# One tiling fewer on TensorE: full-array matmuls issued as two halves of 64 columns

## The chip, the core and the metric

The kernel runs on one core of one Trainium2 chip. The core has a matmul engine (TensorE, called PE in the profile; its weight loads are listed apart as PEld), a vector engine (DVE), a scalar engine (ACT), a general engine (POOL) and a queue engine (SP) that here only issues DMA transfers. Matmuls write to PSUM, which has eight banks of 512 fp32 columns on 128 partitions; DVE and ACT copy ("evict") results from there to the on-chip memory. The metric is the device time of one execution in microseconds (us), a median of three runs for the kernel before. A profiled execution is a run of its own with its own time.

## What is computed

`x` is 8 x 4224 x 192 in fp32. The first part is a causal convolution along the sequence with 7 taps; the 192 channels form 8 groups of 24, and each group has its own softmax-normalised taps. The second part mixes tokens. Cut to what matters:

```python
x = conv(x, softmax(weight))                 # 7 taps, one set for each group of 24 channels
wq, wk = x @ w_q, x @ w_k                    # 192 -> 64 each
W_tok = (1 / sqrt(64)) * einsum('bsd,btd->bst', wq, wk)
mixed = einsum('bst,btd->bsd', W_tok, x)     # no softmax between
out = maximum(mixed, 0) @ w_out              # 192 -> 192
```

As nothing nonlinear stands between the two einsums, `mixed` equals `wq @ (w_k.T @ (x.T @ x))` up to the scale. The kernel uses this: it forms the 192 x 192 Gram matrix `x.T @ x` of each batch and never the 4224 x 4224 token matrix.

## The kernel before, in words

All matmuls are in bf16. Work goes batch by batch through these steps, each an operation on PE with an eviction behind it on ACT or DVE:

- `conv` (`gen_conv`, L559): the sequence is cut into 35 chunks of 122 outputs. For each of 8 channel groups a banded 128 x 128 matrix (`band`) multiplies the loaded chunks (`xw`), 9, 8, 18 or 17 chunks at once. Result: `y`, tokens on partitions.
- `tr_lo` and `tr_hi` (L598, L633): transposes of `y` through PE; the lower 128 channels take the full array, the upper 64 go to one half of the PE columns each for two parts of the sequence. Results: `ytl`, `yth`.
- `wq` (L658, L662): the queries, two blocks of 512 tokens side by side on the two column halves. Result: `wqt`.
- `gram` (L694): three matmuls per chunk on column halves, accumulated in an eighth PSUM bank over the whole batch. Then `turn` (L720) and `m` (L737), the small products with `w_k` that make the mixing matrices `msb` and `mbd`.
- `mix_lo` (L784), on the two row halves of the array, and `mix_hi` (L795), full array; their evictions apply the maximum with zero and write `rt`.
- `fin_hi` (L835, row halves) and `fin_lo` (L853, full array): the product with `w_out`, 128 tokens at a time. The stationary operand is `rt`, of which each matmul takes every fourth column, so that one partition of the output holds four rows that follow each other. `out_sb` is evicted (L869) and stored by SP (L877).

So PE is used in three tilings: 128x128 (full), 128x64 (`COL2`, two column halves that hold their own weights and take their own streams) and 64x128 (`ROW2`, two row halves). A short last block of 128 tokens uses 64x64 once per batch.

The order on each engine is not written by hand. Each operation is added with a planned length, what it needs, how many PSUM banks it takes (of seven) and a turn `vt`. `Planner.plan` places operations one after the other: on each engine, of those that are ready, the one with the smallest `vt`. `vt` comes from a formula of batch and position and an offset per kind from the table `TURN`. For PE, an operation in another tiling than the last one is ranked `STAY` = 0.8 later, waits of up to `HOLD` = 1 ns are accepted for one in the same tiling, and a change costs `SWITCH` = 95 ns of planned time. `Program.place` then writes each engine's stream with semaphore waits for what is not known to be done.

At the start, POOL issues the loads of `x`, which convert to bf16 on the way: batch 0 in four groups, each other batch in two, with a semaphore per group. SP issues nine transfers for the three weight matrices (`emit_weights`, L503) once the third load of batch 0 is in. They share one semaphore. Ten ACT copies (`cast`, L508) convert them to bf16; each of `wq`, `m`, `fin_hi` and `fin_lo` needs all ten (`*casts`). DVE makes the taps, and PE sums the bands with an identity as weights (`collect`, L423).

Of the kernel before, what the change touches and what calls it, by code (L numbers as in the profile page):

```python
# [8 lines left out]
BF16 = mybir.dt.bfloat16  # L9
F32 = mybir.dt.float32  # L10

FULL, COL2, ROW2 = "128x128", "128x64", "64x128"


class Op:


    n = 0

    def __init__(self, engines, emit, ns, needs=(), after=(), banks=0, drains=None, vt=0.0, mode=FULL, tail=0.0):  # L20
        self.engines = (engines,) if isinstance(engines, str) else tuple(engines)
        self.emit = emit

        self.ns = ns

        self.needs = [x for x in needs if x is not None]

        self.after = [x for x in after if x is not None]
        self.banks = banks

        self.drains = drains
        self.vt = vt
        self.mode = mode
        self.tail = tail
        self.users = 0
        self.bank = None
        self.engine = None
        self.end = None

        self.lands = 0.0  # L40

        self.size = 0
        Op.n += 1
        self.id = Op.n


class Planner:
# [1 line left out]


    LAT = {"PE": 240.0, "ACT": 145.0, "DVE": 140.0, "POOL": 150.0, "SP": 0.0}
    SWITCH = 95.0

    STAY = 0.8

    HOLD = 1

    def __init__(self, nbank, first_bank):
        self.ops = []
# [163 lines left out]
def bass_lightweight_conv__then__hypermixer_token_mlp_kernel(  # L223
# [87 lines left out]
    def bank(i, n=1):  # L311
        return PS[:, i * 512 : (i + n) * 512]


    TURN = {
        None: -0.36, "conv": -0.39, "fin_hi": 0.2, "fin_lo": -0.13, "g": -0.29, "gram": 0.01, "gt": 0.37,
        "m": -0.33, "mix_hi": 0.08, "mix_lo": -0.01, "ms": 0.64, "out": -0.7, "rh": -0.7, "rt": 0.7,
        "tr_hi": -0.04, "tr_lo": 0.25, "turn": 0.08, "wq": 0.02, "wqt": 0.3, "y": 0.08, "yth": 0.19,
        "ytl": 0.7,
    }  # L320

    def add(*a, dma=None, kind=None, **k):
        op = Op(*a, **k)
        op.dma = dma
        op.kind = kind
        op.vt += TURN.get(kind, 0.0)
        return planner.add(op)

    def evac_ns(cols, fast=1):
        return {"ACT": 56 + cols / 1.2, "DVE": 62 + cols / (0.96 * fast)}  # L330

    both = ("ACT", "DVE")


    S_W = semaphore("s_w")
# [7 lines left out]
    )  # L343

    one = add("DVE", lambda e, op: e.memset(IDENT[:, :], 1.0), 100, vt=-9.5)
    zero_yt = add("DVE", lambda e, op: e.memset(YTH[64:128, wq_cols[-2] :], 0.0), 100, vt=-8.52)
    zero_b = add("DVE", lambda e, op: e.memset(BAND[:, :, CW:128], 0.0), 80, vt=-8.9)
    zero_x0 = add("DVE", lambda e, op: e.memset(XW[0 : KC - 1, :, 0, :], 0.0), 800, vt=-8.8)
# [56 lines left out]
    for h0, nh in ((0, HB), (HB, HB)):  # L405
        fill, acc = None, None
        for k in range(KC):
            part = PARTS[:, at_part : at_part + CW * nh]
            at_part += CW * nh
            made = add(  # L410
                "DVE",
                lambda e, op, part=part, k=k, h0=h0, nh=nh: e.tensor_tensor(
                    part.rearrange("p (j h) -> p j h", h=nh),
                    IDENTW[:, k : k + CW, :],
                    WSB[:, k, h0 : h0 + nh].unsqueeze(1).to_broadcast([128, CW, nh]),
                    ALU.mult,
                ),
                360, needs=[wn, identw], vt=-7 + 0.1 * k + 0.2 * h0,
            )

            def collect(e, op, part=part, k=k, fill=fill):
                to = op if fill is None else fill
                return e.matmul(  # L423
                    bank(to.bank)[:, 0 : part.shape[1]], IDENT[:, :], part, start=k == 0, stop=k == KC - 1, skip_group_check=True
                )

            acc = add(
                "PE", collect, CW * nh / 2.4, needs=[made, ident], after=[acc], banks=1 if k == 0 else 0, vt=made.vt
            )
            fill = fill or acc  # L430
        done = add(
            "ACT",
            lambda e, op, h0=h0, nh=nh, fill=fill: e.copy(  # L433
                BAND[:, h0 : h0 + nh, 0:CW], bank(fill.bank)[:, 0 : CW * nh].rearrange("p (j h) -> p h j", h=nh)
            ),
            56 + CW * nh / 1.2,
            needs=[acc],
            drains=fill,
            vt=made.vt,
        )  # L440
        out_first.append(acc)
        for h in range(h0, h0 + nh):
            band_done[h] = done
# [47 lines left out]
        gen_load(0, gi)  # L491


    S_C = semaphore("s_c")
    QS, KS, OS = slice(0, DH), slice(DH, 2 * DH), slice(2 * DH, 2 * DH + D)

    def emit_weights(e, op):
        pairs = []
        for t, n, cols in ((wq_t, DH, QS), (wk_t, DH, KS), (wo_t, D, OS)):
            pairs.append((WLO[:, cols], bass.AP(t, 0, [[n, LO], [1, n]])))  # L500
            for p in (0, HI):
                pairs.append((WHI[p : p + HI, cols], bass.AP(t, LO * n, [[n, HI], [1, n]])))
        return [(e.dma_start(d, s), 16) for d, s in pairs]  # L503

    load_c = add("SP", emit_weights, 5000, needs=load[0, 2], dma=("c", S_C, 16 * 9), tail=2500, vt=-3)

    def cast(dst, src, more=()):
        return add("ACT", lambda e, op: e.copy(dst, src), 250, needs=[load_c, *more], vt=-4)  # L508

    def twice(ap):  # L510
        return ap.unsqueeze(1).to_broadcast([ap.shape[0], 2, DH])

    casts = [
        cast(WQL[:, :], WLO[:, QS]),
        cast(WQH[0:HI, 0, :], WHI[0:HI, QS], [zero_q]),
        cast(WQH[HI:128, 1, :], WHI[HI:128, QS], [zero_q]),
        cast(WKL[:, :, :], twice(WLO[:, KS])),
        cast(WKT[0:64, :, :], twice(WLO[0:64, KS]), zero_k),
        cast(WKM[0:64, :, :], twice(WLO[64:128, KS])),
        cast(WKM[64:128, :, :], twice(WHI[64:128, KS])),  # L520
        cast(WKB[64:128, :, :], twice(WHI[64:128, KS]), zero_k),
        cast(WOL[:, :], WLO[:, OS]),
        cast(WOH[:, :], WHI[:, OS]),
    ]

    for b in range(1, B):
# [17 lines left out]
    def gen_conv(b, gi):  # L544
# [6 lines left out]
        for hp in range(H // 2):  # L551
            vt = b + c0 / NCC - 0.15 + 0.02 * hp

            def conv(e, op, hp=hp):
                last = None
                for i in range(2):
                    h = 2 * hp + i
                    o = op.bank * 512 + i * gap
                    last = e.matmul(  # L559
                        PS[:, o : o + n * GRP],  # L560
                        BAND[:, h, :],
                        XW[:, b, c0 : c0 + n, GRP * h : GRP * h + GRP],
# [21 lines left out]
    def gen_transpose(b, cs):  # L584
# [8 lines left out]
        def tr_lo(e, op):  # L593
            ps = bank(op.bank).bitcast(BF16)
            last = None
            for c in cs:
                w, o = width[c], c * CW - t0
                last = e.transpose(ps[:, o : o + w], Y[0:w, yb, c, 0:LO], IDENT[0:w, 0:w])  # L598
            return last

        mm_l = add("PE", tr_lo, 57 * n, needs=needs, after=free, banks=1, vt=vt, kind="tr_lo")
# [10 lines left out]
    def gen_transpose_hi(b, j):  # L612
# [20 lines left out]
                    last = e.transpose(ps[64 * i : 64 * i + HI, o : o + w], Y[0:w, yb, c, LO:D], IDENT[0:w, 0:w])  # L633
            return last

        mm = add("PE", tr_hi, 55 * max(len(p) for p in parts), needs=needs, after=free, banks=1, vt=vt, mode=COL2, kind="tr_hi")
        y_read.setdefault((b, "all"), []).append(mm)
        return add(
            "DVE",
# [5 lines left out]
    def gen_wq(b, j):  # L645
# [8 lines left out]
        def wq(e, op):  # L654
# [9 lines left out]
                )  # L664
            return last

        mq = add("PE", wq, mm_ns(n, 2), needs=[*{id(r): r for c in cs for r in yt_done[b, c]}.values(), turned, *casts],
            after=wfree, banks=1, vt=vt, mode=COL2, kind="wq")
        yth_read[b, j] = [mq]
        for c in cs:  # L670
            for g in range(0, NCC, 8):
# [10 lines left out]
    def gen_gram(b, cs, first, last, before, begun):  # L682
# [18 lines left out]
                    )  # L701
            return mm

        a = add("PE", gram, 84 * len(cs), needs=[*needs, *before], after=begun, vt=vt, mode=COL2, kind="gram")
        y_read.setdefault((b, "all"), []).append(a)
        return [a]

    def gen_mix_weights(b, grams):
# [3 lines left out]
        def copy(dst, src):  # L712
# [4 lines left out]

        turn = add(
            "PE",
            lambda e, op: e.transpose(bank(op.bank).bitcast(BF16)[:, 0:LO], GSB[:, 64:D], IDENT[:, :]),  # L720
            60, needs=[g_read, ident], banks=1, vt=vt, kind="turn")
        turned = add(
            both,
# [3 lines left out]
        def m(e, op):  # L727
# [6 lines left out]
                (WKB, GSB[:, 0:64], LO),  # L734
            )
            for k, (wk, rhs, o) in enumerate(steps):
                last = e.matmul(  # L737
                    bank(op.bank)[:, o : o + rhs.shape[1]],
                    wk[:, :, :].rearrange("p t e -> p (t e)"),
                    rhs,  # L740
# [4 lines left out]
            return last  # L745

        gsb_read = mm = add(
            "PE", m, 290, needs=[g_read, turned, *casts], after=m_read.get(b - 2, []), banks=1, vt=vt, kind="m")
        mb = b % 2
        old = m_read.get(b - 2, [])  # L750

# [17 lines left out]
    def gen_mix(b, j, evm, evq):  # L769
# [5 lines left out]
        n_out += 1  # L775
        free = rt_read.get(n_rt - 1 - NRT, [])
        ofree = store_of[n_out - 1 - NOUT] if n_out > NOUT else out_first
        vt = b + 1.2 + t0 / S * 0.95 + (TURN.get(None, 0.0) if b == B - 2 else 0.0)
        nt = n // 128

        def mix_lo(e, op):
# [9 lines left out]
            return last  # L791

        def mix_hi(e, op):
            p = 64 * nh
            return e.matmul(  # L795
                bank(op.bank)[0:p, 0:n], MBD[0:p, mb, 0:p], WQT[0:p, wqb, q0 : q0 + n], start=True, stop=True
            )

        ml = add("PE", mix_lo, mm_ns(n), needs=[*evm, evq], after=free, banks=nh, vt=vt, mode=ROW2, kind="mix_lo")
        mh = add("PE", mix_hi, mm_ns(n), needs=[*evm, evq], after=free, banks=1, vt=vt, mode=FULL if nh == 2 else "64x64", kind="mix_hi")  # L800
        m_read.setdefault(b, []).extend([ml, mh])
        wq_read[b, j] = [ml, mh]

# [23 lines left out]
        for q in range(0, nt, step):  # L827
# [15 lines left out]
                return last  # L843

            fvt = vt + 0.05 + 0.02 * q
            fh = add("PE", fin_hi, mm_ns(D, step), needs=[rl, rh, *casts], after=ofree, banks=nh, vt=fvt, mode=ROW2, kind="fin_hi")

            def fin_lo(e, op, iq=iq, q=q, fh=fh):
                last = None
                for i in iq:  # L850
                    for a in range(nh):
                        o = (i - q) * D
                        last = e.matmul(  # L853
                            bank(fh.bank + a)[:, o : o + D],
                            RT[:, slot, a, i:n:nt],
                            WOL[:, :],
# [3 lines left out]
                        )  # L860
                return last

            fl = add("PE", fin_lo, mm_ns(D, step * nh), needs=[rl, rh, *casts], after=[fh], vt=fvt + 0.001, kind="fin_lo")
            readers += [fh, fl]

            def ev_out(e, op, q=q, fh=fh):
# [91 lines left out]
```

## Time and profile before

| | |
|---|---|
| median of 3 runs | 177.99 us (177.98 to 179.53) |
| profiled execution | 178.53 us, of which span 176.8 us |
| PE busy | 161.5 us (91%), 2454 matmuls |
| PE weight loads | 112.3 us, 2454 |
| DVE busy, ACT busy | 123.5 us (70%), 122.6 us (69%) |
| granted TensorE clock, mean | 0.993 |
| DMA | 40.26 MB, mean 228 GB/s |
| PE share of the chain that ended last | 81% |

The span goes from the first to the last instruction of the profiled execution; the remaining 1.7 us lie around it. In a timeline a row has a start, a length, an engine, a line, an operation, what is written from what, sizes, and a count where several alike are merged; in brackets stands the idle time of the engine before it and what ended it. The length of a matmul contains its way through the array, so matmuls overlap in the listing: the distance between starts tells how fast they follow each other, not the length.

### The profile page before, as it was taken

How to read it: one execution, taken by the hardware profiler on the slowest of the kernel's cores; microseconds unless marked ns; L12 is line 12 of the kernel's file. 1: busy time of each engine (PE TensorE's matmuls, PEld its weight loads, DVE VectorE, ACT ScalarE, POOL GpSimd, SP SyncE). 2: the span in 40 equal slices, each digit the busy share in tenths (PEclk: the TensorE clock that was granted, in tenths of full speed). 3: DMA queues.
4: the chain of work that ended last, by engine and by line, in shares of the span. 5: the costliest groups of instructions: out<-in, count | busy, mean ns of one | idle time of the engine just before them, and what ended most of it. 6: DMA issues, size and time to landing. Idle time of an engine off the chain costs nothing.

```text
span 176.8 us, 5567 instructions
## 1 busy us (share of the span) xinstructions
PE 161.5 (91%) x2454; PEld 112.3 (64%) x2454; DVE 123.5 (70%) x219; ACT 122.6 (69%) x209; POOL 30.3 (17%) x39
## 2 busy tenths in 40 slices
PE   0589849999999999999999999999999999999880
PEld 0249737676766777767686577666775778666440
DVE  5948776887567477677969866797658775887660
ACT  4054364957789996797768767587779846968870
POOL 7999731525230000000000000000000000000000
PEclk9999999999999999999999999999999999999997
DMA  3999999999999999999999995530844075556697
GB/s 30 160 190 189 197 197 190 190 194 191 212 318 312 249 230 333 248 307 232 286 283 233 322 266 203 231 151 4 352 185 180 28 296 226 233 237 279 257 398 287
DMA packets 48151, 40.26 MB, mean 228 GB/s; under 512 B 37632, under 2 KB 40960, under 8 KB 48128
## 3 DMA queue, kind: packets, MB, share of 16 engines
q0 software_dynamic: 36128, 13.61, 64.7%
q1 hardware_dynamic: 12000, 26.31, 39.9%
q8 instruction: 19, 0.31, 0.7%
q14 instruction: 4, 0.03, 0.0%
HBM read 27.56 MB, written 25.95 MB: 303 GB/s over the span
## 4 chain that ended last, share of the span: by engine, by line
PE 81%; DMA 8%; ACT 3%; SPq 2%; POOL 2%; issue 1%; POOLq 0%
PE ps L853 15%; PE ps L694 14%; PE ps L559 11%; PE ps L835 9%; PE ps L598 7%; DMA xw<-in_x_dram 5%; PE ps L633 5%; PE ps L784 5%; PE ps L658 5%; PE ps L795 5%; PE ps L662 4%; DMA whi<-in_moe_w_out_dram 3%; SPq L503 2%; POOL xw L479 1%; ACT out_sb L869 1%
## 5 line engine op out<-in xcount | busy, mean ns | idle before, releaser
L869 DVE COPY out_sb<-ps 128x768 f32<-128x768 f32 (+1 forms) x36 | 32.0, 891 | 25.4 <-PE ps L853 25.3
L807 ACT ACTIVATE rt<-ps 128x1024 bf16<-128x1024 f32 (+3 forms) x50 | 37.9, 770 | 14.0 <-PE ps L784 13.4
L578 ACT CAST y<-ps 122x864 bf16<-122x864 f32 (+3 forms) x49 | 36.9, 793 | 8.1 <-PE ps L559 7.6
L869 ACT COPY out_sb<-ps 128x768 f32<-128x768 f32 (+1 forms) x36 | 26.6, 746 | 10.7 <-PE ps L853 10.2
L694 PE MATMUL ps<-y 122*64 122x128 bf16 (+2 forms) x840 | 34.0, 222 | 0.0
L479 POOL DMA_DIRECT2D xw<-in_x_dram x34 | 29.9, 908 | 19.4 <-issue 18.6
L694 PEld LDWEIGHTS ps<-y 122*64 122x64 bf16 x840 | 28.0, 110 | 8.1 <-issue 7.6
L559 PE MATMUL ps<-xw,band 128*128 128x432 bf16 (+3 forms) x144 | 31.4, 323 | 0.8 <-ACT band L433 0.7
L853 PE MATMUL ps<-wol,rt 128*128 128x192 bf16 x264 | 30.5, 250 | 0.0
L853 PEld LDWEIGHTS ps<-wol,rt 128*128 128x128 bf16 x264 | 21.0, 116 | 7.8 <-issue 2.9
L578 DVE CAST y<-ps 122x816 bf16<-122x816 f32 (+3 forms) x23 | 20.6, 912 | 3.9 <-PE ps L559 3.6
L605 DVE COPY ytl<-ps 128x976 bf16<-128x976 bf16 (+1 forms) x40 | 23.0, 589 | 0.6 <-PE ps L598 0.2
L808 DVE TENSOR_SCALAR rt<-ps 128x512 bf16<-128x512 f32 (+3 forms) x30 | 20.1, 681 | 4.7 <-PE ps L784 2.7
L598 PE MATMUL ps<-ident,y 122*128 122x122 bf16 x280 | 20.5, 216 | 0.4 <-DVE y L578 0.4
L835 PE MATMUL ps<-woh,rt 64*128 64x192 bf16 x264 | 20.0, 250 | 1.0 <-ACT rt L807 0.7
L598 PEld LDWEIGHTS ps<-ident,y 122*128 122x128 bf16 x280 | 17.5, 97 | 4.4 <-ACT y L578 0.6
L640 DVE COPY yth<-ps 128x512 bf16<-128x512 bf16 (+1 forms) x40 | 14.9, 378 | 5.5 <-PE ps L633 5.1
L633 PE MATMUL ps<-ident,y 122*64 122x122 bf16 (+1 forms) x344 | 17.0, 217 | 0.0
L559 PEld LDWEIGHTS ps<-xw,band 128*128 128x128 bf16 x144 | 11.4, 97 | 7.8 <-issue 2.2
L658 PE MATMUL ps<-ytl,wql 128*64 128x512 bf16 (+1 forms) x72 | 14.6, 368 | 1.9 <-ACT woh L508 1.9
L835 PEld LDWEIGHTS ps<-woh,rt 64*128 64x128 bf16 x264 | 11.3, 114 | 7.9 <-ACT rt L807 1.5
L678 ACT CAST wqt<-ps 128x512 bf16<-128x512 f32 (+1 forms) x24 | 12.4, 532 | 5.2 <-PE ps L662 4.7
(63 smaller groups left out, 128.0 us busy)
## 6 DMA issues: line engine op xcount, KB each, us to landing
out_dram<-out_sb SPq DMA_DIRECT2D x28, 768.0 KB, 5.0
xw<-in_x_dram POOLq DMA_DIRECT2D x7, 816.0 KB, 30.3
xw<-in_x_dram POOLq DMA_DIRECT2D x7, 768.0 KB, 35.6
out_dram<-out_sb SPq DMA_DIRECT2D x8, 384.0 KB, 3.1
xw<-in_x_dram POOLq DMA_DIRECT2D x2, 432.0 KB, 8.3
out_dram<-out_sb SPq DMA_DIRECT2D x8, 96.0 KB, 3.6
xw<-in_x_dram POOLq DMA_DIRECT2D x1, 384.0 KB, 5.1
xw<-in_x_dram POOLq DMA_DIRECT2D x8, 45.8 KB, 23.8
```

Source lines behind the costliest of these rows:

```text
L479: lambda e, op, part=part: e.dma_start(*part),
L559: last = e.matmul(PS[:, o : o + n * GRP], BAND[:, h, :], XW[:, b, c0 : c0 + n, GRP * h : GRP * h + GRP], start=True, stop=True,)
L578: return e.copy(dst, src) if op.engine == "ACT" else e.tensor_copy(dst, src)
L598: last = e.transpose(ps[:, o : o + w], Y[0:w, yb, c, 0:LO], IDENT[0:w, 0:w])
L605: lambda e, op: e.tensor_copy(YTL[:, t0:t1], bank(mm_l.bank).bitcast(BF16)[:, 0:cols]),
L633: last = e.transpose(ps[64 * i : 64 * i + HI, o : o + w], Y[0:w, yb, c, LO:D], IDENT[0:w, 0:w])
L658: last = e.matmul(ps[64 * i : 64 * i + DH, 0:n], WQL[:, :], YTL[:, t0 + i * n : t0 + (i + 1) * n], start=True, stop=False)
L694: mm = e.matmul(bank(GB)[p : p + 64, o : o + z - r], Y[0:w, yb, c, r : r + 64], Y[0:w, yb, c, r:z], start=st, stop=end, skip_group_check=True,
L807: return e.activation(dst, src(), AF.Relu)
L835: last = e.matmul(bank(op.bank + a)[:, o : o + D], RT[64 * a : 64 * a + HI, slot, 2, i:n:nt], WOH[64 * a : 64 * a + HI, :], start=i == q, ...
L853: last = e.matmul(bank(fh.bank + a)[:, o : o + D], RT[:, slot, a, i:n:nt], WOL[:, :], start=False, stop=True, skip_group_check=True,)
L869: return e.copy(dst, src) if op.engine == "ACT" else e.tensor_copy(dst, src)
```

## The change

1. The constant for the full tiling is gone. New helpers `halves` and `turn_halves` issue what was one full-array matmul or transpose as two, each with 64 of the weight columns and 64 of the output partitions, and both with the same moving operand. They are used in `collect`, `conv`, `tr_lo`, `turn`, `m` and `fin_lo`. `mix_hi` becomes two matmuls in column halves, and its short form one; that one now reads all 128 partitions, so a part of `wqt` is cleared first (`zero_w`). PE is then used in two tilings, 128x64 and 64x128.
2. The nine weight transfers become three operations of three, each with a semaphore of its own, issued when the second load of batch 0 is in. `wq` needs the casts of `w_q` alone, `m` those of `w_k`, `fin_hi` and `fin_lo` those of `w_out`.
3. The formulas for `vt` are no longer used: each of the 1005 operations takes its `vt` from a table, `TURNS`, by its place in the list. `SWITCH` is 145, `STAY` 0.788 and `HOLD` 23.

```diff
-FULL, COL2, ROW2 = "128x128", "128x64", "64x128"
+TURNS = [
+    int(t) / 1000
+    for t in """
+-9360 -9860 -8870 -8880 -9260 -9160 -9060 -8960 -8910 -8910 -8860 -9360 -9360 -8360 -8260 -8360 -8160
...
+""".split()
+]
+
+COL2, ROW2 = "128x64", "64x128"
...
-    SWITCH = 95.0
-
-    STAY = 0.8
-
-    HOLD = 1
+    SWITCH = 145.0
+
+    STAY = 0.788
+
+    HOLD = 23
...
-        op.vt += TURN.get(kind, 0.0)
+        op.vt = TURNS[len(planner.ops)]
...
+    def halves(e, out, lhsT, rhs, **k):
+
+        e.matmul(out[0:64], lhsT[:, 0:64], rhs, **k)
+        return e.matmul(out[64:128], lhsT[:, 64:128], rhs, **k)
+
+    def turn_halves(e, out, in_, identity):
+        e.transpose(out[0:64], in_[:, 0:64], identity)
+        return e.transpose(out[64:128], in_[:, 64:128], identity)
...
+    zero_w = add("DVE", lambda e, op: e.memset(WQT[64:128, :, wq_cols[-2] :], 0.0), 150, vt=-8.51)
...
-    load_c = add("SP", emit_weights, 5000, needs=load[0, 2], dma=("c", S_C, 16 * 9), tail=2500, vt=-3)
...
+        return add("SP", emit, 1700, needs=load[0, 1], dma=(name, semaphore(f"s_{name}"), 16 * 3), tail=4000, vt=vt)
+
+    load_q = gen_weight("wq", wq_t, DH, QS, -3.0)
+    load_k = gen_weight("wk", wk_t, DH, KS, -2.9)
+    load_o = gen_weight("wo", wo_t, D, OS, -2.8)
...
-                    last = e.matmul(
+                    last = halves(
+                        e,
                         PS[:, o : o + n * GRP],
                         BAND[:, h, :],
                         XW[:, b, c0 : c0 + n, GRP * h : GRP * h + GRP],
...
-                last = e.transpose(ps[:, o : o + w], Y[0:w, yb, c, 0:LO], IDENT[0:w, 0:w])
+                last = turn_halves(e, ps[:, o : o + w], Y[0:w, yb, c, 0:LO], IDENT[0:w, 0:w])
...
-            p = 64 * nh
-            return e.matmul(
-                bank(op.bank)[0:p, 0:n], MBD[0:p, mb, 0:p], WQT[0:p, wqb, q0 : q0 + n], start=True, stop=True
-            )
+            last = None
+            for i in range(nh):
+                last = e.matmul(
+                    bank(op.bank)[64 * i : 64 * i + HI, 0:n],
+                    MBD[:, mb, 64 * i : 64 * i + HI],
+                    WQT[:, wqb, q0 : q0 + n],
+                    start=True,
+                    stop=True,
+                )
+            return last
...
-                        last = e.matmul(
+                        last = halves(
+                            e,
                             bank(fh.bank + a)[:, o : o + D],
                             RT[:, slot, a, i:n:nt],
                             WOL[:, :],
```

## The prediction

> **What bounds the kernel now.** I read the page's busy shares first, then the same by stretches, then the tensor engine's timeline, the start-up, and the last microseconds. The page and its slices:
>
> ```profile
> PE 161.5 (91%) x2454; PEld 112.3 (64%) x2454; DVE 123.5 (70%) x219; ACT 122.6 (69%) x209; POOL 30.3 (17%) x39
> ...
> PE   0589849999999999999999999999999999999880
> ```
>
> The stretches (time in each, then each engine's busy time, then the granted clock, DMA share and GB/s):
>
> ```profile
> 22.00:26.00 4.00, 2.00 (x48) 1.33 (x44) 3.37 (x7) 2.33 (x10) 1.11 (x3) 1.00 1.58 194
> 26.00:30.00 4.00, 3.76 (x80) 2.85 (x81) 1.97 (x4) 1.73 (x5) 0.93 (x1) 1.00 1.61 193
> 30.00:40.00 10.00, 10.00 (x162) 6.88 (x158) 8.39 (x14) 7.59 (x13) 4.03 (x5) 1.00 1.60 192
> 40.00:60.00 20.00, 20.00 (x319) 14.07 (x316) 13.41 (x20) 16.71 (x28) 4.78 (x6) 1.00 1.42 251
> ```
>
> From 30 to 160 us PE is busy all the time and DVE and ACT are not: PE sets the end, except before 30 us and after 160 us. "Busy" hides something, though: a matmul's modelled end includes some 0.17 us of pipeline, so short gaps do not show. The starts show them:
>
> ```profile
> 71.80 0.52 PE L835 MATMUL ps<-woh,rt 64*128 64x192 bf16 x8
> 72.16 0.38 PE L784 MATMUL ps<-wqt,msb 64*128 64x512 bf16 x2
> 72.48 0.85 PE L853 MATMUL ps<-wol,rt 128*128 128x192 bf16 x8
> 73.16 0.38 PE L795 MATMUL ps<-wqt,mbd 128*128 128x512 bf16 x1
> 73.47 0.63 PE L694 MATMUL ps<-y 122*64 122x192 bf16 x15
> ```
>
> A lone 512-column matmul streams for 0.215 us (below). L795 starts at 73.16, and the next, in another tiling, at 73.47: 0.31, so 0.095 is lost where the tiling changes. L784 to L853 (64x128 to 128x128) is 0.32: 0.10 lost. By the starts of single matmuls over the whole trace, a change costs 93 ns for full to column halves, 93 for row halves to full, 96 for column to row halves, and 99 for row to column halves (three cases only). Nothing hides this, since weights and streams both stop.
>
> Do halves run side by side? These do:
>
> ```profile
> 66.39 0.41 PE L658 MATMUL ps<-ytl,wql 128*64 128x512 bf16 x2
> 66.63 0.38 PE L662 MATMUL ps<-yth,wqh 128*64 128x512 bf16 x2
> 66.84 0.38 PE L658 MATMUL ps<-ytl,wql 128*64 128x512 bf16 x2
> 67.06 0.38 PE L662 MATMUL ps<-yth,wqh 128*64 128x512 bf16 x2
> ```
>
> Each row is two 512-column matmuls, one per column half, starting 4 ns apart; the next pair follows after 0.215 us, as after one full 512-column matmul.
>
> At the start, PE waits for weights:
>
> ```profile
> 13.19 0.33 SPq L503 DMA_DIRECT2D wlo<-in_moe_w_q_dram  x1
> 23.55 0.24 ACT L508 CAST wql<-wlo 128x64 bf16<-128x64 f32 x1 [1.59 <-DMA whi<-in_moe_w_out_dram]
> 25.84 0.35 ACT L508 CAST woh<-whi 128x192 bf16<-128x192 f32 x1
> 26.24 0.41 PE L658 MATMUL ps<-ytl,wql 128*64 128x512 bf16 x2 [1.90 <-ACT woh L508]
> ```
>
> All nine weight transfers share one semaphore and the first query matmul waits for all ten casts, the output weights' too.
>
> **The change, part by part.** The sum is made against the profiled execution, 178.53 us (span 176.8); the runs' median, 177.99, is 0.54 lower, and the difference is applied to it.
>
> *Tiling changes.* In the built programs' PE order, tilings change 152 times before (128x128, 128x64, 64x128 and, for the last short block, 64x64) and 94 times after, 47 in each direction. Before: 152 x 94 ns = 14.3 us; after: 47 x 96 + 47 x 99 = 9.2. I take -5.1 us. Nearly all lie in the saturated stretch, so all of it counts.
>
> *Streams.* Full matmuls become 782 more matmuls and weight loads, but two halves share the time of one. Starts: full transposes (L598) 53 ns apart; pairs of column-half transposes (L633) 53 ns per pair; L853 82.5 ns steady, its 192 columns alone. Adding the columns streamed per column half in program order gives 137.8 us before, 137.6 after: -0.2.
>
> *First load after a tiling change.* The second matmul after a change comes late, as its weights were not loaded in advance: by 27 ns at L853 (110 against 83) and L835, 24 ns in column halves (236 against 213), 10 ns for packed weights in the full tiling. Summed over the trace this is about 3.1 us before (1.2 in the full tiling, 1.0 in row halves, 0.9 in column halves). After, 47 starts in row halves cost about 0.9, as most begin with L835. The 47 in column halves mostly begin with L853's weights, taken every fourth column of rt; that load in this tiling is in no row. Bounds: 24 ns, the packed load in column halves, or that scaled by what striding did in the full tiling. Taking 3 ns of each load as hidden (an estimate), 10 and 27 ns stand for loads of 13 and 30, and 24 for 27; 27 x 30/13 = 62, so 59 ns late. That is 1.1 to 2.8 us. I take the upper one, as the stride is L853's own: +0.6 in all; the lower gives -1.1.
>
> [...]
>
> *Start.* The transfers go by the second input load (landed 10.8 us by the semaphore's updates) instead of the third (13.17), so SP issues them 2.3 us earlier; nothing else is in SP's queue then. Query casts wait for three transfers alone. Issued by about 12.4, landing 5 us later as now, they are cast by about 18.5. In the new order the first query matmul has 10.6 us of PE work ahead of it; the old one started 9.3 us behind its work at 18.4 us, so this one comes at about 20, after its weights. The old gap at 26.24 (2.0 us beyond the tiling change) goes. Next late is the input: batch 1's first load lands at 20.16, where PE would ask at about 20.3; moving weights (192 KB of output weights at 190 GB/s, 1.0 us) ahead of it may delay it by 0 to 1.0, priced at 0.3. ACT stands behind the output weights until about 21 us; only batch 1's evictions queue there, not due sooner. DVE gets one more clearing before the softmax: clearings there start 0.18 us apart, +0.2. Sum -1.5; bounds -2.0 and 0 (if PE then waits for inputs).
>
> *Order.* The table replaces the vt of every operation, and the planner takes SWITCH 145, STAY 0.788, HOLD 23. PE's waits in mid-kernel are small: by starts against streams, 1.8 us from 30 to 160 us, and about 2.5 us after 160, where few operations are left. Counting PE work between a matmul and the user of its evicted result, 76 operations have under 1.2 us of it before and 79 after (425 and 422 from 30 us on). I take 0; the ends are -2 (half of these waits gone) and +4 (mid-kernel waits tripled). ACT and DVE keep the same evictions; their 246 us over two engines leave a quarter of a 170 us span free. The last evictions and stores, some 4 us from the last matmul to the end, stay.
>
> Sum: -5.1 - 0.2 + 0.6 - 1.5 = -6.2; 172.3 for the profiled execution, **171.8 us** by the median.
>
> **Rivals.**
> *The strided half loads bind (slower).* If L853's halves load in turn, at 62 ns each, a pair takes 124 ns instead of 82.5: 264 x 41.5 ns = +11.0, giving 182.8. It decides between faster and slower from 82.5 + 6200/264 = 106 ns a pair. Against it: after a change both column halves restart 24 ns late, not one by twice that, so packed loads run side by side; L835 hides two strided 128-column loads in 82 ns. For it: no row has a strided load in column halves. 8%. A quarter of that effect still gives 174.6.
> *The new order waits more.* PE saves time only if DVE and ACT bring results sooner by as much; queued evictions could give back 3 to 4 us in place of tiling changes: 175.3. Against: shares of 70%. 14%.
> *Halves do not overlap for the convolution.* L559 streams 24-column pieces of xw; two such streams at once are in no row. If they took turns, its 22.8 us double: 194.6. Against: L694's halves stream overlapping parts of y. 2%.
> *The start gains nothing, inputs binding:* 173.3, inside the forecast's own range.
> *The order also removes waits, first loads at their lower price:* -6.2 - 2.0 (waits) - 1.7 (loads) - 0.5 (start) = -10.4, 167.6. 14%.
>
> **How the numbers follow.** Forecast (169 to 174) 62%; 14% at 175.3; 14% near 167.6; 8% and 2% at the slow ends. Range 167 to 176.5, which leaves out the two slow mechanisms and part of the fringes. About 1% (1.8 us) is what a measurement can tell here: the three runs go from 177.98 to 179.53. Over 1% faster is below 176.2: 0.84; within 1%: 0.06, from the order's and half-load cases' edges; slower: 0.10.
>
> **What would show it.** Tiling changes still 95 to 100 ns each and 94 of them; pairs of L853's halves 82 to 83 ns apart, of transposes 53; the first query matmul near 20 us and no 2 us gap after it; last matmul near 166 us instead of 172. The prediction is wrong if pairs are further apart than this, if PE's idle time names DVE or ACT much oftener between 30 and 160 us, or if a convolution pair takes more than 0.19 us.

## The result and the profile after

The changed kernel takes 180.61 us (median of 4, 180.24 to 181.05) beside 178.30 us for the kernel before (median of 4, 177.98 to 179.53): a ratio of 1.013, with a 95% interval of 1.0084 to 1.0177. It is 1.3% slower, where 171.8 us was forecast, and it lies outside the range. The profiled execution took 180.53 us, with a span of 178.8 us.

The page of the changed kernel: busy times, two rows of the slices, and the row of the DMA queue that the page calls instruction (packets, MB, share of time):

```profile
PE 159.0 (89%) x3236; PEld 121.3 (68%) x3236; DVE 128.0 (72%) x226; ACT 118.2 (66%) x203; POOL 30.3 (17%) x39
...
PE   0689499999889999999999979999999999999940
...
PEclk9999979999999999999999999999999999999995
...
q8 instruction: 25, 0.41, 0.9%
```

The same row of the kernel before:

```profile
q8 instruction: 19, 0.31, 0.7%
```

There are 782 more matmuls, as the change says. Before, PE's row of slices was full from the seventh slice up to the last three. Now there is a hole in the fifth slice (18 to 22 us), smaller ones later, and the granted clock drops in the sixth. The stretches of the changed kernel (length, then busy time of PE, PEld, DVE, ACT and POOL, then granted clock, DMA share, GB/s):

```profile
18.00:22.00 4.00, 1.45 (x51) 1.34 (x46) 1.01 (x3) 1.79 (x8) 1.67 (x2) 0.95 1.50 207
22.00:26.00 4.00, 4.00 (x68) 3.48 (x67) 2.33 (x4) 0.57 (x3) 1.96 (x4) 0.62 1.61 194
...
40.00:60.00 20.00, 18.54 (x403) 14.60 (x401) 13.38 (x24) 14.12 (x25) 4.63 (x6) 1.00 1.46 238
60.00:80.00 20.00, 19.96 (x418) 15.62 (x420) 16.24 (x27) 13.94 (x24) 0.00 (x0) 1.00 1.34 275
80.00:110.00 30.00, 28.24 (x582) 21.22 (x577) 21.27 (x34) 21.98 (x38) 0.00 (x0) 1.00 1.12 255
```

PE is idle for 2.55 us of the first row, 1.46 of the third and 1.76 of the last. What it waits for, from the view of the waits of PE (in total, times, longest):

```profile
PE ps L391 <- issue: 2.6, 1, 2.6
...
PE ps L915 <- issue: 1.0, 1, 1.0
PE ps L767 <- issue: 0.7, 1, 0.7
PE ps L386 <- issue: 0.7, 1, 0.7
```

The word is "issue" each time: no semaphore and no other engine. These stops are in the middle of an operation. The timeline around the longest one:

```profile
18.98 0.22 PE L390 MATMUL ps<-ident,y 122*64 122x122 bf16 x1
19.02 0.27 PE L391 MATMUL ps<-ident,y 122*64 122x122 bf16 x2
21.84 0.26 PE L391 MATMUL ps<-ident,y 122*64 122x122 bf16 x1 [2.55 <-issue]
```

PE stops between two transposes of one operation. Where the stops stand gives the cause away. In the order of PE's own records (weight loads, matmuls and the 38 semaphore waits among them), they come at numbers 448, 1472, 1728, 3008, 3264, 3520 and 3776, with small ones at 1984, 2240 and 2752: every one is 192 plus a multiple of 256. The instruction queue has 25 packets of 16,384 bytes for PE's 6,472 loads and matmuls, one for each 259, and in the kernel before 19 for 4,908, one for each 258. The reading of these numbers that the experiments below put to the test: a packet holds the next 256 of PE's instructions, and PE stops at the border between two such pieces when the next has not come. From the records of instructions and of packets (times in us; "needed" is when PE reaches the border, "goes on" when it starts the next instruction; the last two columns count from where PE reached the border before, and "asked" is the start of the packet, as the request itself is in no record):

```
kernel, border      packet from - to   needed   goes on   since the border before, packet asked after
before, 1216         42.75 -  43.70     47.94    48.00     8.0   2.9
before, 1472         50.97 -  51.91     56.22    56.28     8.3   3.0
after,   448         19.48 -  20.45     19.07    21.84     3.8   4.2
after,  1472         44.28 -  45.17     45.72    46.66     5.4   4.0
after,  1728         51.34 -  52.27     52.83    53.79     7.1   5.6
after,  3008         82.76 -  83.71     84.69    85.19     6.1   4.2
after,  3776        102.59 - 103.53    103.55   104.95     5.9   4.9
```

While `x` is loaded (until 106 us), a packet takes 0.9 to 1.0 us, and PE goes on 1.4 to 1.6 us after its end where it had stopped. In this stretch the packet starts 3.2 to 6.8 us after PE reached the border before, 4.5 on average. The large values are those behind a stop, which they contain: counted from where PE went on, all lie between 3.2 and 4.7 us, 4.0 on average. By these three times (an estimate), PE stops here when it works through 256 instructions in less than about 4.0 + 0.95 + 1.45 = 6.4 us, on average. In the kernel before, 256 of them are 7.2 to 9.3 us of work and the packet starts 3.3 us after the border on average; each comes in time. Only the piece up to number 448 is shorter, 6.3 us, and its packet lands 1.6 us ahead of need, the least of all. In the changed kernel 256 are 5.8 us of work on average, 3.8 up to the first stop. The excess over 0.1 us at the borders up to 108 us adds up to 7.0 us.

To this comes the clock. After the first stop it is at 0.62 on average from 22 to 26 us, and at 0.50 from 21.60 to 25.00. The transposed pairs, 53 ns apart at a clock of 1.00, come 101 ns apart up to 23.4 us. Taking the work from 21.84 to about 24.7 us as stretched to twice its time gives 1.4 us more, an estimate. 180.5 - 7.0 - 1.4 = 172.1 us is an estimate of what the profiled execution would have taken without either, if each stop is lost time in full; the forecast for that execution was 172.3.

### The profile page after: what moved, and what is told of

Read it like the earlier page. It is cut to its first block, busy times and chain, and to the rows that moved or that the text cites. A ratio compares the mean times of both kernels' runs of the same rounds, so it can differ in the third digit from the quotient of the medians.

```text
span 178.8 us, 7128 instructions
## 1 busy us (share of the span) xinstructions
PE 159.0 (89%) x3236; PEld 121.3 (68%) x3236; DVE 128.0 (72%) x226; ACT 118.2 (66%) x203; POOL 30.3 (17%) x39
## 4 chain that ended last, share of the span: by engine, by line
PE 87%; issue 4%; DVE 3%; ACT 2%
PE ps L386 26%; PE ps L767 14%; PE ps L915 9%; PE ps L387 7%; PE ps L706 6%; PE ps L858 5%; PE ps L390 5%; PE ps L391 4%; PE ps L731 4%; PE ps L735 4%; PE ps L870 4%; ACT wqt L751 1%; DVE out_sb L950 1%; ACT rt L887 1%; ACT out_sb L950 0%
## 5 line engine op out<-in xcount | busy, mean ns | idle before, releaser
L651 ACT CAST y<-ps 122x816 bf16<-122x816 f32 (+3 forms) x45 | 34.2, 784 | 17.6 <-PE ps L387 16.4
L767 PE MATMUL ps<-y 122*64 122x64 bf16 (+2 forms) x840 | 34.3, 222 | 0.8 <-issue 0.7
L767 PEld LDWEIGHTS ps<-y 122*64 122x64 bf16 x840 | 31.2, 112 | 3.9 <-issue 1.4
L386 PE MATMUL ps<-wol,rt 128*64 128x192 bf16 x264 | 31.5, 255 | 0.7 <-issue 0.7
L387 PE MATMUL ps<-wol,rt 128*64 128x192 bf16 x264 | 31.5, 255 | 0.0
L386 PE MATMUL ps<-xw,band 128*64 128x432 bf16 (+3 forms) x144 | 30.6, 324 | 0.7 <-ACT band L499 0.7
L387 PE MATMUL ps<-xw,band 128*64 128x432 bf16 (+3 forms) x144 | 30.8, 325 | 0.0
L651 DVE CAST y<-ps 122x864 bf16<-122x864 f32 (+3 forms) x27 | 24.9, 932 | 6.8 <-PE ps L387 6.6
L386 PEld LDWEIGHTS ps<-wol,rt 128*64 128x64 bf16 x264 | 22.9, 138 | 7.6 <-issue 3.5
L888 DVE TENSOR_SCALAR rt<-ps 128x512 bf16<-128x512 f32 (+3 forms) x36 | 23.8, 667 | 1.2 <-PE ps L858 0.9
L391 PE MATMUL ps<-ident,y 122*64 122x122 bf16 x280 | 22.2, 220 | 2.6 <-issue 2.6
L387 PEld LDWEIGHTS ps<-wol,rt 128*64 128x64 bf16 x264 | 22.8, 138 | 0.8 <-issue 0.8
L390 PE MATMUL ps<-ident,y 122*64 122x122 bf16 x280 | 22.1, 220 | 0.0
L390 PEld LDWEIGHTS ps<-ident,y 122*64 122x64 bf16 x280 | 18.4, 112 | 4.3 <-issue 2.7
L391 PEld LDWEIGHTS ps<-ident,y 122*64 122x64 bf16 x280 | 18.2, 112 | 0.1
```

Source lines behind the costliest of these rows:

```text
L386: e.matmul(out[0:64], lhsT[:, 0:64], rhs, **k)
L387: return e.matmul(out[64:128], lhsT[:, 64:128], rhs, **k)
L390: e.transpose(out[0:64], in_[:, 0:64], identity)
L391: return e.transpose(out[64:128], in_[:, 64:128], identity)
L651: return e.copy(dst, src) if op.engine == "ACT" else e.tensor_copy(dst, src)
L767: mm = e.matmul(bank(GB)[p : p + 64, o : o + z - r], Y[0:w, yb, c, r : r + 64], Y[0:w, yb, c, r:z], start=st, stop=end, skip_group_check=True,
```

## The experiments

Two theories stood against each other. *Supply*: the change is worth what was forecast, and the stops come from the arrival of instructions, 256 at a time, late because of the loads of `x` and felt because the halves use up 256 sooner. *Order*: the stops belong to the new order (a buffer, a bank or a queue that the profile doesn't show), whatever the number of instructions.

### Without the loads of batches 1 to 7

Both kernels, with this edit:

```diff
+    skip = {x.id for (b, gi), ops in load.items() if b for x in ops}
     for op in planner.order:
+        if op.id in skip:
+            continue
+        op.needs = [x for x in op.needs if x.id not in skip]
         program.place(op)
...
-                        XW[:, b, c0 : c0 + n, GRP * h : GRP * h + GRP],
+                        XW[:, 0, c0 : c0 + n, GRP * h : GRP * h + GRP],
```

> The kernel before, with the loads of batches 1 to 7 left out; their convolutions read batch 0's input instead, so only one eighth of the input transfers remain and the results of batches 1 to 7 are those of batch 0. Order of instructions on PE, ACT and DVE as before. Fetch theory (PE's instructions arrive in pieces of 256, through DMA engines that the input loads keep busy until 106 us; a piece comes 6 to 7 us after the last one was begun, and the kernel before uses one up in 7 to 9.7 us): nothing much to gain here, 175.5 to 178 us. Order theory (the lost time comes from the new order of operations): the same, 175.5 to 178 us. It is the reference for the next run.

> The changed kernel with the same loads left out. Fetch theory: the seven gaps at multiples of 256 PE instructions (6.9 us together in the changed kernel's profile) and the half clock after the first of them (1.4 us) vanish, and the time is 170.5 to 172.5 us, 5 to 6 us below the kernel before with the same loads left out; pieces start within 1 us of the previous piece's end. Order theory: the order on each engine is that of the changed kernel, so its gaps stay and the time stays at 178 to 181 us, no faster than the kernel before with the same loads left out.

Measured: the kernel before 177.17 us (ratio to its own full version 0.992, 0.9889 to 0.9951), the changed kernel 170.87 us (ratio to the kernel before with its loads 0.9572, 0.9515 to 0.9629). Both lie in the ranges that the supply theory gave. Without loads the change is a gain of 6.3 us, and no stop at a border is left. Stretches of the changed kernel without loads:

```profile
18.00:22.00 4.00, 4.00 (x123) 3.81 (x119) 3.60 (x7) 2.41 (x7) 0.00 (x0) 1.00 0.01 4
22.00:26.00 4.00, 4.00 (x73) 2.76 (x70) 3.30 (x7) 3.29 (x8) 0.00 (x0) 1.00 0.02 6
...
40.00:60.00 20.00, 20.00 (x434) 15.42 (x432) 14.73 (x23) 16.00 (x28) 0.00 (x0) 1.00 0.42 165
```

PE's matmuls and weight loads are the same but for the operand of the convolutions; 11 semaphore waits are gone. The packets now start 0.8 us after the border before on average (2.3 at most) instead of 4.5. PE comes to number 448 as fast as with loads, 3.7 us behind the border before, but its packet runs from 15.62 to 16.55 us and PE needs it at 18.47. The loads cost the kernel before 1.1 us and the changed kernel 9.7, of which the stops and the half clock are 8.4.

### The borders moved

72 very small matmuls at the head of PE's stream of the changed kernel, ahead of the bands:

```diff
+            e.wait_ge(sem, value)
+            for k in range(72):
+                e.matmul(bank(0)[0:64, 0:16], MBD[:, 0, 0:64], MBD[:, 0, 0:16], start=True, stop=True)
             for f in program.streams["PE"]:
                 f(e)
```

> The changed kernel with 72 small extra matmuls (144 PE instructions) ahead of PE's first work, while PE waits for the bands anyway. Everything behind them is as in the changed kernel. Fetch theory: the borders of the pieces move 144 to 145 instructions forward in the work, so the first piece is asked for before 12 us instead of 15.3; the gap of 2.7 us at 19.07 shrinks to at most 1.4 us, the clock between 22 and 26 us stays full, and every other gap stands 145 instructions earlier in the order than it did; 176 to 178.5 us. Order theory: gaps stay at the same operations, 180 to 181 us.

Measured: 178.34 us (177.95 to 178.92), 0.9983 of the kernel before (0.9947 to 1.002): more instructions, and 2.3 us less than the changed kernel, as the supply theory had it. The stop at 19 us is gone, and another stands in the convolutions, which ran through before:

```profile
22.39 0.34 PE L387 MATMUL ps<-xw,band 128*64 128x432 bf16 x1
24.18 0.34 PE L386 MATMUL ps<-xw,band 128*64 128x432 bf16 x1 [1.45 <-issue]
```

All stops are again at 192 plus a multiple of 256, which is 145 records earlier in the work; they sum to 4.7 us. So no instruction and no operation owns a stop. The first one is shorter as its border falls elsewhere in the dense stretch, and the clock holds (the stretch from 22 to 26 us):

```profile
22.00:26.00 4.00, 2.55 (x53) 1.77 (x47) 2.24 (x4) 1.00 (x2) 2.00 (x3) 1.00 1.59 188
```

The small matmuls are not free: they push the bands back, and the convolutions behind the last band start at 14.76 us instead of 13.31. With 2.3 us less of stops and 1.4 less of half clock, 1.45 more at the start leaves a gain of some 2.3, the one measured.

### More instructions in the kernel before

The convolutions cut along the sequence in 2 or 4 matmuls, `fin_lo` (and `mix_lo`) in two along the columns that are streamed: 728 more matmuls and weight loads, with the tilings and the order of the kernel before.

```diff
-                        PS[:, o : o + n * GRP],
-                        BAND[:, h, :],
-                        XW[:, b, c0 : c0 + n, GRP * h : GRP * h + GRP],
+                    parts = 4 if n > 9 else 2
+                    edges = [n * i // parts for i in range(parts + 1)]
+                    for u, v in zip(edges, edges[1:]):
...
+                            XW[:, b, c0 + u : c0 + v, GRP * h : GRP * h + GRP],
```

> The kernel before with 728 more matmuls and as many weight loads, and nothing else: the streams of conv are cut in four (two for the short ones), those of fin_lo and mix_lo in two, in the old tilings and the old order. Each cut costs 2.5 ns of its own, 1.8 us in all. Fetch theory: 256 instructions now last about 6.3 us as in the changed kernel, so gaps of 2 to 5 us in all appear at multiples of 256 PE instructions before 106 us and none after; 181 to 185 us. Order theory: nothing but the cuts themselves, 179.5 to 180.5 us, with no gaps at those places.

Measured: 180.54 us (180.03 to 181.16), a ratio of 1.0106 (1.0042 to 1.017). This falls between the two expectations, so the time alone decides nothing. The trace does more: the kernel before has no stop at a border above 0.2 us; now there are four, at 448, 1216, 1728 and 2496, with 1.7 us in all. From PE's waits:

```profile
PE ps L858 <- issue: 0.8, 1, 0.8
...
PE ps L562 <- issue: 0.5, 2, 0.3
```

There are fewer stops than in the changed kernel, as 256 instructions are 6.2 us of work on average here (5.1 up to the first stop, then 5.6 or more) and the extra ones lie in other places. For the cuts themselves the kernel before gives a size: its convolutions of 216 columns follow each other after 92.5 ns (12.96 to 14.26 us), those of 432 after 182 (20.88 to 21.42), so a cut costs some 3 ns, where 2.5 was taken. The first 1.9 us of added time can't be seen in the total: PE waited that long for `woh` in the kernel before, and no longer does.

### Loads held back

The opposite remedy, slower loads: from batch 2 on the loads in pieces of 6 chunks, each issued only when the one two places ahead of it has landed.

```diff
+                cut = [(c1 + i, min(6, m - i)) for i in range(0, m, 6)]
...
+    for i in range(2, len(chain)):
+        chain[i].needs.append(chain[i - 2])
```

> The changed kernel, all input loaded, but from batch 2 on the loads go in pieces of at most 6 chunks instead of 16 or 17, and each piece is issued only when the last but one has landed, so that at most two pieces (about 0.6 MB, some 3 us of transfers) stand ahead of an instruction fetch. Order on PE, ACT and DVE as in the changed kernel. Fetch theory: fetches start 0.5 to 3 us after the previous piece's end instead of 3.2 to 5.6, the gaps after 30 us (4.2 us in all) go, the first gap and the half clock stay: 175.5 to 177.5 us. A rival within it: it is the share of time in which the input queue is not empty that counts, not how much stands in it; then the waits stay near 4 us, loads last longer, and the time stays at 179.5 to 182 us.

> The same with the 72 small matmuls ahead of PE's first work. Fetch theory: the first gap shrinks as it did with these matmuls alone (1.6 us at 22.4 us, no half clock) and the later ones go: 173.5 to 175.5 us, faster than both kernels. Rival (only the share of time with a filled queue counts): 177.5 to 180 us.

> The kernel before with its loads in the same pieces from batch 2 on. Fetch theory: its instruction pieces arrived 2.8 us or more ahead of need, so there is nothing to gain: 177.5 to 179 us, unless a load comes late for its convolution (then slower). Rival (pacing helps by itself, through the stores or otherwise): 174 to 177 us.

Measured: 196.01, 192.76 and 193.62 us (ratios 1.0946, 1.0731 and 1.0769): all far above what was expected, because the pace was too slow. In the first of the three, the slices from 24 to 48 us moved 103 to 131 GB/s where the changed kernel had 191 to 193, the loads lasted until 144 us, and PE waited for input; from the waits of the first of the three:

```profile
PE ps L388 <- issue: 7.1, 3, 5.8
PE ps L388 <- DMA xw<-in_x_dram: 6.3, 4, 3.9
```

The long wait in the first line, 5.8 us, is no stop at a border: it ends at 136.95 us, before a convolution, 0.1 us after a load has landed. So the word "issue" alone doesn't mean that instructions are missing; the place does.

As remedies they failed. Of the cause they show this much: the packets' wait went down from 4.5 to 2.8 us on average, and three borders with a stop were left instead of eight, one of them the first (2.5 us at 19.35). But waits of 4.6 us and more also occur behind the slower loads. What in the DMA engines makes a packet wait, the number of transfers queued or the bytes in flight, stays open.

### Fewer instructions while the loads run

The changed kernel in its own order, with `fin_lo` as one full-array matmul in batches 0 to 4, alone and with the 72 small matmuls ahead:

```diff
-    def halves(e, out, lhsT, rhs, **k):
-
+    def halves(e, out, lhsT, rhs, split=True, **k):
+        if not split:
+            return e.matmul(out, lhsT, rhs, **k)
...
                             WOL[:, :],
+                            split=b >= 5,
```

> The changed kernel in its own order, with the output product on the low 128 channels (fin_lo) as one full-array matmul instead of two halves for batches 0 to 4: 165 matmuls and 165 weight loads fewer in the stretch in which the input is still being loaded, and one tiling change more in each of some 27 blocks, for which the spacings of these kernels give about 65 ns each: +1.8 us of work. Theory (PE's instructions come 256 at a time, and each piece arrives too late while the loads run): 256 instructions last about 6.8 us instead of 5.4 to 6.5, and the stops at 45, 52, 84, 91, 97 and 103 us, together 4.2 us, shrink to less than 1.5 us; the first stop of 2.7 us at 19 us and the half clock behind it stay, since no such block has run by then. 178.5 to 180 us against 180.6 for the changed kernel. Rival (the number of instructions per microsecond doesn't matter, the stops come from the order): the stops stay and the work is added: 182 to 183 us.

> The kernel above with 72 very small matmuls ahead of PE's work, which move every border between two pieces of 256 instructions 145 instructions earlier in the work, as in the run that did this to the changed kernel alone (178.34 us). Theory: its stop of 1.6 us at 22 us stays, the later stops (0.82, 0.42, 0.56, 0.26 and 0.85 us, some 3 us together) shrink to under 1 us, the added tiling changes cost 1.8 us: 176.5 to 178 us, at or below the kernel before. Rival: nothing shrinks, 180 us.

Measured: 178.59 us (178.38 to 179.5) and 177.24 us (176.77 to 178.25); ratios to the kernel before 1.0004 (0.9966 to 1.0041) and 0.9955 (0.9926 to 0.9983). Both as the supply theory had it, and some 3 to 4 us under its rival. 330 instructions fewer and a third tiling back in the stream make the changed kernel faster by 2.0 us. All PE waits of the first of the two on "issue":

```profile
PE ps L392 <- issue: 2.7, 1, 2.7
...
PE ps L768 <- issue: 0.4, 1, 0.4
```

The first stop is as it was, since no `fin_lo` has run by then, and the clock is at 0.58 behind it. Of the later ones, 4.3 us in the changed kernel, 0.7 is left. From 60 to 106 us, 256 instructions are 6.7 us of work on average here instead of 6.0, above the 6.4 worked out earlier. The second kernel is the only one with all its loads that is below the kernel before, by 0.8 us; it has two stops left (1.6 us at 22.7 and 1.0 at 35.9).

### The old order

The changed kernel with `vt` by the old formula, `TURN` and all, instead of the table, and the new `SWITCH`, `STAY` and `HOLD`; 102 tiling changes instead of 94. With and without the loads of batches 1 to 7.

```diff
-        op.vt = TURNS[len(planner.ops)]
+        op.vt += TURN.get(kind, 0.0)
```

> The changed kernel with its order taken from the kernel before: the due time of each operation by the old formula instead of the table, the new prices of a tiling change kept. PE's stream has 102 tiling changes instead of 94. Theory (halves and two tilings are worth what was forecast, and the lost time is the supply of instructions, which the order table doesn't touch): the same stops at the same places of 256, 0.8 us for 8 more changes and what the old order waits for data: 180.5 to 183.5 us. Rival (the table itself is what costs time, by waits it brings in): below 179 us.

> The kernel above without the loads of batches 1 to 7 (every convolution reads batch 0's input), as was done with both kernels earlier: the changed kernel took 170.87 us so, the kernel before 177.17. Theory: without loads no stop is left at the borders, and the order is seen alone: 8 changes at 95 ns and some waits, 171.5 to 174 us; so halves and two tilings without the table are worth 3 to 5.5 us of the 6.3. Rival (most of the 6.3 us is the table's): above 175 us.

Measured: 180.12 us (179.68 to 180.56; ratio 1.0113, 1.0083 to 1.0143) with the loads, 0.4 below the expectation's lower end, and 173.31 us (172.92 to 174.31) without. With loads, halves in the old order are as slow as with the table: the stops are there (4.8 us, all at such borders), at other places of the work. So the table does not make them. Without loads the table is worth 173.31 - 170.87 = 2.4 us, and halves, two tilings and the earlier weights in the old order 177.17 - 173.31 = 3.9. With loads, all of the 2.4 us is gone (180.12 us in the old order, 180.61 with the table); by the supply theory, an order that keeps PE busier only reaches the border sooner.

## Why the prediction was wrong

**The step that failed** is the first sentence of *Streams*: "Full matmuls become 782 more matmuls and weight loads, but two halves share the time of one." It is right of the array (transposed pairs 53 ns apart, pairs of `fin_lo` 80 to 83, in the changed kernel) and was taken for the whole cost. The 1,564 instructions more came with 25 packets of the instruction queue instead of 19, and PE stopped at some of the borders between them. That term was set to nothing; it measured 7.0 us of stops and 1.4 us of half clock, 8.4 in the profiled execution. No rival had it, and so the range was too narrow.

The profile of before could have shown the margin. Its queue q8 has 19 packets for 4,908 loads and matmuls, one for each 258; the packets' records give a wait of 2.4 to 4.3 us under the loads and a length of 0.95. A third more instructions in the 160 us between PE's first work and the forecast last matmul make 256 of them last 6.3 us on average, and less where transposes crowd, against some 5 us from one border to the end of the late packets. The 1.45 us from a packet's end to the next instruction can't be seen before anything stops, so a size would have been a guess; a rival with a chance of its own would not. None of the prediction's signs of being wrong names such a wait: pairs, convolutions and waits on DVE or ACT came out as it said.

The other steps, by what they named:

- *Tiling changes.* 94 of them. Without loads, the starts after a change against the end of the streams before give 104 ns for column to row halves and 91 for the way back, 9.2 us in all, as forecast. Right.
- *Halves.* `fin_lo` in the changed kernel, first pair behind a tiling change:

```profile
104.95 0.35 PE L915 MATMUL ps<-woh,rt 64*128 64x192 bf16 x4 [1.03 <-issue]
105.24 0.30 PE L386 MATMUL ps<-wol,rt 128*64 128x192 bf16 x1
105.24 0.30 PE L387 MATMUL ps<-wol,rt 128*64 128x192 bf16 x1
105.37 0.25 PE L386 MATMUL ps<-wol,rt 128*64 128x192 bf16 x1
105.38 0.25 PE L387 MATMUL ps<-wol,rt 128*64 128x192 bf16 x1
105.45 0.25 PE L386 MATMUL ps<-wol,rt 128*64 128x192 bf16 x1
105.46 0.25 PE L387 MATMUL ps<-wol,rt 128*64 128x192 bf16 x1
105.54 0.25 PE L386 MATMUL ps<-wol,rt 128*64 128x192 bf16 x1
```

  Both halves start within 10 ns, and pairs follow after 80 to 83 ns; transposed pairs come 53 ns apart at full clock and pairs of convolutions of 432 columns about 182. So the rivals of binding strided loads and of convolutions that do not overlap are out.
- *First load after a tiling change.* The second pair above comes 0.13 us behind the first instead of 0.08: some 50 ns late (53 on average over the 44 such starts without loads), where 59 was taken and 24 the other end. Right in kind, nearly in size; the 3 ns of each load that the 59 takes as hidden were the author's estimate, and no run shows them.
- *Start.* The casts of `wq` start at 17.5 us, about when forecast (18.5 for the end). The first query matmul came at 24.33 us, not near 20: the stop at 19 and the half clock stand ahead of it. Without loads it comes at 19.8. The wait of 1.9 us for `woh` is gone, as forecast, and the time went into the stop in the same place.
- *Order.* Taken as nothing, with -2 as one end. The table is worth 2.4 us without loads, some 0.8 of it in eight tiling changes fewer. Part of it can be seen at the end: the kernel before loses 2.0 us after 160 us in five waits of 0.26 to 0.55 (L784, L795, L835), the changed kernel 0.6 in two.
- *Last matmul* near 166 us: it came at 171.8.

The agreement of 6.2 forecast with the 6.3 us of the runs without loads is better than its terms. In these runs the kernel before waits 0.2 us for `woh` instead of 1.9, so the start is worth less there than in the sum, and the order more. What is shown is the size of the whole; the start and the order were not measured apart under the loads, where the stops cover both.

## What to carry to other kernels

In these kernels the instructions were traffic of their own: 19 packets of the instruction queue for 4,908 loads and matmuls, 25 for 6,472. Before a matmul is split, count PE's loads and matmuls to one packet (258 in the kernel before), see from the packets how long after a border the next one starts in the busiest DMA stretch (2.4 to 4.3 us there), and compare this, with the packet's length (0.95 us) behind it, with the shortest time in which PE will use up as many (3.8 us in the changed kernel). The 1.4 to 1.6 us from a packet's end to PE's next instruction came on top here; the kernel before, in which no packet was late, does not show them. The signs here were stops marked "issue" at equal distances in PE's count, 192 plus multiples of 256, which stood 145 records earlier in the work when 72 matmuls were put in ahead. What helped here was fewer and longer matmuls where loads ran (178.59 us against 180.61); without loads the halves were the faster ones (170.87 against 177.17).

## What the runs showed of the hardware

- The packet for the next border started at the earliest 0.3 us before PE reached the border before (kernel before, 152.29 us) and 0.1 us after it in the changed kernel (158.06 us). In the changed kernel it started 0.8 us after PE reached that border on average in the run without loads, and 4.5 under loads (4.0 after PE went on), with some 190 to 310 GB/s moved; PE went on 1.4 to 1.6 us after the packet's end when it had to wait.
- First stops with 2.0 to 2.7 us of idle PE were followed by a granted clock of 0.58 to 0.66 over the 4 us from 22 us on: 2.55 us and 0.62 in the changed kernel, 2.7 and 0.58 with whole `fin_lo`, 2.0 and 0.66 in the old order. Two with 1.4 to 1.45 us (72 small matmuls ahead, alone and with whole `fin_lo`) were followed by 1.00. The length alone doesn't decide: the kernel before idled 1.90 us up to 26.24 us, and its clock was 1.00 from 26 to 30 us.
- In the changed kernel, column halves took strided 64-column weights for both halves every 80 to 83 ns (105.37 to 105.95 us), and packed ones every 53 ns where the clock was 1.00.
